# Second-pass output products of a gated MLP: from plain matmuls to Strassen's seven

## Chip, cores and metric

One NeuronCore of a Trainium2 chip runs the whole program; inputs and outputs lie in HBM. The metric is the device time of one execution in microseconds; the kernel before took 1191.15 us (median of three runs, 1191.02 to 1193.08).

## What is computed

The reference is block-causal attention (8 batches, 8 heads, 576 positions, head size 64) whose output, as 4608 tokens of 512, goes through a gated MLP with d_ff 1536:

```python
scores = (1.0 / np.sqrt(D)) * np.matmul(q, k.transpose(0, 1, 3, 2))
mask = pos[:, None] // 64 >= pos[None, :] // 64
attn = softmax(np.where(mask, scores, -1e9))        # over the last axis
x = np.matmul(attn, v).transpose(0, 2, 1, 3).reshape(B * S, H * D)
gate = 1.0 / (1.0 + np.exp(-(x @ w_gate)))
val = x @ w_val
out = (gate * val @ w_out).astype(np.float32)
```

The weights arrive as float64, which the kernel reads as pairs of 32-bit words and turns into float32 itself. For accuracy every product of two float32 matrices is made of three matmuls of a high and a low part (high·high, high·low, low·high), so each operand is split: ACT makes the high part by a cast, DVE or POOL the low part by a subtraction.

## The kernel before, in words

The d_ff axis is cut in 12 chunks of 128. The first four (F1) are computed batch by batch beside attention (`mlp1`, L577 and on; `hidden` L121, `out_mm` L129), and their contribution to the output is written to `part_d` in DRAM. The other eight are computed after attention, in two passes g = 0 and 1 of four chunks each. A pass runs over six blocks of 768 tokens (NK = 6, two halves of N2 = 384).

In a block the hidden products are made by Strassen's scheme with seven products in place of eight. A `unit` (L862) is one of four combinations of column half q and gate or value; it has seven `product`s (L844) of six matmuls 128×384 (L852), and DVE adds the PSUM banks and the copied first product p1 (L868) together at L883 to L896. The value unit multiplies by one plus the tanh of the gate's half (L875, L879), which gives a quarter of h; ACT and DVE or POOL split it (`split_h`, L857, L859 and L860) into `hH2` and `hL2`.

Then `out_block` (L917) multiplies h with w_out plainly: six tiles of 128 tokens, each 12 matmuls 128×512 (L926), 72 a block. In pass 0 ACT scales the tile by one half (L935) and it is stored to `part2_d`. In pass 1 POOL adds the tiles of `part_d` and `part2_d` (L948), DVE scales the product and adds that sum (L949), and SP stores the result (L950). The last block fetches all its part sums early (`parts_load`, L900) and writes in halves at L941.

While a block runs, the x of the next is fetched (`x_load`, L715), three combinations of it are made by POOL (`x_sums`, L728) and the seven operands are split (`x_split`, L735): ACT casts (L742) and DVE subtracts (L743) four, two and one operands at a time for each of two row halves. During pass 0, `later` holds pieces of work for pass 1: combining and splitting the gate and value weights (`combine`) and splitting w_out (`wo_piece`, L705), each written to DRAM and read back at the turn of the pass.

The order on each engine is set at build time by a scheduler that simulates the program; `behind` adds constraints of order only. Each engine works through its queue in order. PSUM has two banks in `ps_m` (tiles m) and six in `ps_b` (tiles b).

Of the kernel before, what the change touches and what calls it, by code (L numbers as in the profile page):

```python
# [9 lines left out]
F32 = mybir.dt.float32  # L10
# [30 lines left out]
def attn_glu_kernel(ctx: ExitStack, tc: tile.TileContext, q, k, v, w_gate, w_val, w_out, out):  # L41
# [117 lines left out]
    with ExitStack() as s2:  # L159
# [468 lines left out]
        wo_d = dram.tile([P, 4, 2, DM], F32, name="wo_d")  # L628
# [85 lines left out]
        def x_load(k, j):  # L714

            b, o = divmod(2 * k * N2, S)
            n0 = S - o
            XB = cv.tile([P, 6, N2], F32, name="XB", bufs=2)
# [16 lines left out]
        def x_split(XBs, other=None):  # L735

            def split(a, b, src):
                for j, XB in enumerate(XBs):
                    if src == 2:
                        nc.vector.tensor_sub(out=XB[:, 2], in0=XB[:, 2], in1=XB[:, 5])  # L740
                    x = XB[:, src:src + b - a]
                    nc.scalar.copy(out=XO[j][0][:, a:b], in_=x)  # L742
                    sub = nc.vector.tensor_sub(out=XO[j][1][:, a:b], in0=x, in1=XO[j][0][:, a:b].bitcast(F32))  # L743
                    if other:
                        behind(sub.ins, other)

            split(0, 4, 0)
            split(4, 6, 4)
            split(6, 7, 2)
# [106 lines left out]

        def split_h(q, i, hH, hL, h):  # L857
            f, n = ((q, 0), (q, N2), (q + 2, 0), (q + 2, N2))[i]
            nc.scalar.copy(out=hH[:, f, n:n + N2], in_=h)  # L859
            (nc.vector if q else nc.gpsimd).tensor_sub(out=hL[:, f, n:n + N2], in0=h, in1=hH[:, f, n:n + N2].bitcast(F32))  # L860

        def unit(q, gv, w, ts, hH, hL):  # L862
# [3 lines left out]
            p1 = m2.tile([P, N2], F32, name="p1", bufs=2)  # L866
# [5 lines left out]
            def done(i, c):  # L872
# [4 lines left out]
                else:  # L877
                    h = ts[0] if i == 0 else c
                    nc.vector.scalar_tensor_tensor(out=h, in0=ts[i], scalar=1.0, in1=c, op0=ALU.add, op1=ALU.mult)  # L879
                    split_h(q, i, hH, hL, h)  # L880
# [10 lines left out]
            done(1, c12)  # L891
            done(3, c22)
            done(0, A)
# [6 lines left out]
        def parts_load(k):  # L900

            a = [x.rearrange("p a n -> p (a n)") for x in (cv.tile([P, 6, N2], F32, name="XB", bufs=2) for _ in range(2))]
            a += [cv.tile([P, 2, S], F32, name="KQ", bufs=2).rearrange("p a n -> p (a n)") for _ in range(2)]
            slots = [x[:, j * DM:(j + 1) * DM] for x in a for j in range(x.shape[1] // DM)]
            sums = {}
            n = N2 // P
            for t in (*range(n, 2 * n), *range(n)):
                r = 2 * k * N2 + t * P
                pr = [slots.pop(0) for _ in range(2)]
                for tile_, src in zip(pr, (part_d, part2_d)):  # L910
                    nc.sync.dma_start(out=tile_, in_=src[r:r + P, :])
                nc.gpsimd.tensor_add(out=pr[0], in0=pr[0], in1=pr[1])
                sums[t] = pr[0]
            return sums

        def out_block(g, k, hH, hL, wo, sums=None):
            n = N2 // P  # L917
            last_unit = last2["PE"]
            for ts in (range(n, 2 * n), range(n)):
# [11 lines left out]
                for t in ts:  # L931
                    r = 2 * k * N2 + t * P
                    ost = io.tile([P, DM], F32, name="ost2", bufs=2)
                    if g == 0:
                        nc.scalar.mul(out=ost, in_=po[t], mul=0.5)  # L935
                        nc.sync.dma_start(out=part2_d[r:r + P, :], in_=ost)
                        continue
                    if sums:
                        for e, queue in enumerate((nc.sync, nc.scalar)):
                            c = slice(e * DM // 2, (e + 1) * DM // 2)  # L940
                            nc.vector.scalar_tensor_tensor(out=ost[:, c], in0=po[t][:, c], scalar=0.5, in1=sums[t][:, c],  # L941
                                                           op0=ALU.mult, op1=ALU.add)
                            queue.dma_start(out=out[r:r + P, c], in_=ost[:, c])
                        continue
                    pr = [io.tile([P, DM], F32, name=f"pr{i}", bufs=2) for i in range(2)]
                    for tile_, src in zip(pr, (part_d, part2_d)):
                        mark2("SP", nc.sync.dma_start(out=tile_, in_=src[r:r + P, :]))
                    nc.gpsimd.tensor_add(out=pr[0], in0=pr[0], in1=pr[1])  # L948
                    nc.vector.scalar_tensor_tensor(out=ost, in0=po[t], scalar=0.5, in1=pr[0], op0=ALU.mult, op1=ALU.add)  # L949
                    nc.sync.dma_start(out=out[r:r + P, :], in_=ost)  # L950
# [7 lines left out]
        x_split(early_x, sums)  # L958
# [9 lines left out]
        ps_b = s2.enter_context(tc.tile_pool(name="ps_b", bufs=6, space=PSUM, reuse_waits="tile"))  # L968
        W.update({u: wgv_tile(*u) for u in units[1:]})
# [17 lines left out]
        for n, (q, gv) in enumerate(units):  # L987
            for j in range(KC):
                def one(n=n, q=q, gv=gv, j=j):
                    st = io.tile([P, 2, 7, P], F32R, name="st")  # L990
# [3 lines left out]
        for f in range(4):  # L994
            def one(f=f):
                st = io.tile([P, 2, DM], F32R, name="sto", tag="st")
                wo_piece(1, f, st, True)
                nc.sync.dma_start(out=wo_d[:, f], in_=st.bitcast(F32))
# [8 lines left out]
        hL = hp2.tile([P, 4, 2 * N2], F32R, name="hL2")  # L1007
        for g in range(G):
            for k in range(NK):
                end = g == G - 1 and k == NK - 1  # L1010
                if not end and (g or k):
                    XBs = [x_load((k + 1) % NK, j) for j in range(KC)]
                    for XB in XBs:
                        x_sums(XB, nc.gpsimd)
                sums = parts_load(k) if end else None
                ts = {}
                gens = [unit(q, gv, W[q, gv], ts, hH, hL) for q, gv in units]
# [12 lines left out]
                if not end:  # L1030
                    x_split(XBs)
                out_block(g, k, hH, hL, wo, sums)
                if g + 1 < G:
                    do_later(k, 2)
                    if k == NK - 1:
                        assert not later
                        wo = wop.tile([P, 4, 2, DM], F32R, name="wo2")
                        nc.sync.dma_start(out=wo.bitcast(F32), in_=wo_d)
# [29 lines left out]
```

## Time and profile before

| what | value |
|---|---|
| median of three runs | 1191.15 us |
| profiled execution, its time | 1190.19 us |
| its span (first to last instruction) | 1188.3 us |
| mean granted TensorE clock | 0.995 |
| first multiplication by a tanh of pass 0 (L879) | 637.4 us |
| pass 1 (g = 1), six blocks | 907 to 1183.5 us |
| from the last output matmul's start to the end of the span | 1183.2 to 1188.3 us |

PE is TensorE's matmul stream, PEld its weight loads, which run beside it; DVE, ACT and POOL are the vector, scalar and GpSimd engines, SP issues most DMAs. A row of the timeline is start, duration, engine, line, operation, and "out<-in" in the program's tile names. Matmuls are pipelined, so how long one takes is read from start to start. A line of the chain names what held the end of the program at that time, with the count of instructions in it. A group of the trace gives its total and mean, then the engine's idle time ahead of it and what ended that.

### The profile page before, as it was taken

How to read it: one execution, taken by the hardware profiler on the slowest of the kernel's cores; microseconds unless marked ns; L12 is line 12 of the kernel's file. 1: busy time of each engine (PE TensorE's matmuls, PEld its weight loads, DVE VectorE, ACT ScalarE, POOL GpSimd, SP SyncE). 2: the span in 40 equal slices, each digit the busy share in tenths (PEclk: the TensorE clock that was granted, in tenths of full speed). 3: DMA queues.
4: the chain of work that ended last, by engine and by line, in shares of the span. 5: the costliest groups of instructions: out<-in, count | busy, mean ns of one | idle time of the engine just before them, and what ended most of it. 6: DMA issues, size and time to landing. Idle time of an engine off the chain costs nothing.

```text
span 1188.3 us, 19309 instructions
## 1 busy us (share of the span) xinstructions
PE 1155.9 (97%) x6749; PEld 975.7 (82%) x6749; DVE 762.1 (64%) x1397; ACT 620.8 (52%) x1372; POOL 355.6 (30%) x390
## 2 busy tenths in 40 slices
PE   6899999999999999999999999999999999999998
PEld 4556778778777877787889889899999998998997
DVE  4678855554555546457959976867876755746744
ACT  6777766766676667665335354453454322423421
POOL 2345523222331323134002223223122161451440
PEclk8999999999999999999999999999999999999999
DMA  8655434435434453534424245325288264263351
GB/s 190 183 136 117 108 89 100 114 75 126 101 91 106 100 128 76 119 109 128 132 63 124 89 138 204 111 94 204 66 299 294 81 195 139 76 205 101 120 177 54
DMA packets 253361, 153.34 MB, mean 129 GB/s; under 512 B 193232, under 2 KB 215248, under 8 KB 252624
## 3 DMA queue, kind: packets, MB, share of 16 engines
q1 hardware_dynamic: 241600, 132.15, 39.9%
q10 hardware_dynamic: 11280, 18.91, 4.3%
q8 instruction: 53, 0.87, 0.3%
q0 software_dynamic: 384, 1.05, 0.3%
q14 instruction: 44, 0.36, 0.1%
HBM read 104.73 MB, written 47.33 MB: 128 GB/s over the span
## 4 chain that ended last, share of the span: by engine, by line
PE 81%; DVE 7%; DMA 4%; ACT 3%; issue 2%; POOL 2%; SPq 2%; DVEq 0%; POOLq 0%; ACTq 0%
PE b L852 20%; PE m L126 14%; PE bank L253 14%; PE m L926 10%; PE m L133 7%; PE bank L257 6%; PE b L926 5%; PE bank L126 3%; DMA pr<-part_d 2%; DVE XL L743 1%; ACT P L381 1%; PE bank L133 1%; POOL pr L948 1%; PE m L257 1%; DMA out_dram<-ost 0%
## 5 line engine op out<-in xcount | busy, mean ns | idle before, releaser
L852 PE MATMUL b<-XH,w 128*128 128x384 f32 x1344 | 351.2, 336 | 6.1 <-DVE v L888 3.4
L852 PEld LDWEIGHTS b<-XH,w 128*128 128x128 f32 x1344 | 244.0, 188 | 13.0 <-DVE v L888 6.6
L852 PE MATMUL b<-XL,w 128*128 128x384 f32 x672 | 224.7, 335 | 0.0
L381 ACT ACTIVATE P<-bank,nm 128x512 f32<-128x512 f32 (+3 forms) x256 | 132.2, 531 | 72.7 <-DVE nm L378 72.7
L378 DVE TENSOR_REDUCE nm<-bank 128x2 f32<-128x1024 f32 (+3 forms) x128 | 105.4, 823 | 40.9 <-ACT P L381 37.8
L852 PEld LDWEIGHTS b<-XL,w 128*128 128x128 f32 x672 | 126.1, 188 | 1.3
L926 PE MATMUL m<-wo,hH 128*128 128x512 f32 x384 | 124.9, 391 | 0.0
L356 ACT COPY G<-bank 128x768 f32<-128x768 f32 (+3 forms) x140 | 93.4, 695 | 26.7 <-PE bank L257 25.8
L253 PE MATMUL bank<-G,VS 128*64 128x320 f32 (+4 forms) x896 | 94.5, 360 | 0.1
L133 PE MATMUL m<-wo,hH 128*128 128x512 f32 x256 | 85.4, 398 | 1.4 <-ACT ost L610 1.0
L253 PEld LDWEIGHTS bank<-G,VS 128*64 128x64 f32 x896 | 56.1, 137 | 36.8 <-issue 4.7
L875 ACT ACTIVATE g<-g 128x384 f32<-128x384 f32 x72 | 37.4, 524 | 89.6 <-DVE g L888 58.9
L926 PEld LDWEIGHTS m<-wo,hH 128*128 128x128 f32 x384 | 71.9, 188 | 13.6
L742 ACT CAST XH<-XB 128x1536 fp32r<-128x1536 f32 (+2 forms) x72 | 66.2, 938 | 32.2 <-DVE XB L740 25.6
L126 PE MATMUL m<-XH,wv 128*128 128x512 f32 x240 | 82.3, 400 | 0.0
L126 PE MATMUL m<-XH,wg 128*128 128x512 f32 x240 | 81.8, 398 | 0.0
L743 DVE TENSOR_TENSOR XL<-XB,XH 128x1536 fp32r<-128x1536 f32 (+2 forms) x72 | 77.6, 1083 | 1.6 <-ACT XH L742 1.2
L926 PE MATMUL m<-wo,hL 128*128 128x512 f32 x192 | 75.2, 392 | 0.0
L257 PEld LDWEIGHTS bank<-ident,P 128*128 128x128 f32 x560 | 65.7, 141 | 11.5 <-ACT P L381 0.7
L257 PE MATMUL bank<-ident,P 128*128 128x128 f32 x560 | 74.9, 273 | 0.1
L948 POOL TENSOR_TENSOR pr<-pr,pr 128x512 f32<-128x512 f32 x30 | 40.3, 1344 | 109.2 <-DMA pr<-part_d 107.6
L398 DVE MEMSET bank<- 64x128 f32 x64 | 10.6, 165 | 95.4 <-PE bank L253 94.7
(182 smaller groups left out, 2315.2 us busy)
## 6 DMA issues: line engine op xcount, KB each, us to landing
pr<-part_d SPq DMA_DIRECT2D x60, 256.0 KB
xT_d<-xT ACTq DMA_DIRECT2D x32, 288.0 KB
XB<-xT_d SPq DMA_DIRECT2D x16, 576.0 KB
part_d<-ost SPq DMA_DIRECT2D x36, 256.0 KB
VS<-in_v_dram SPq DMA_DIRECT2D x64, 128.0 KB
part_d<-ost ACTq DMA_DIRECT2D x32, 256.0 KB
rqk<-in_k_dram SPq DMA_DIRECT2D x108, 72.0 KB
rqk<-in_q_dram SPq DMA_DIRECT2D x108, 72.0 KB
```

What stands on the lines that cost most here:

```text
L126: mm = nc.tensor.matmul(ps, lhsT=lh, rhs=rh, start=(i == 0), stop=(i == n - 1))
L133: mm = nc.tensor.matmul(ps, lhsT=lh[:, f, t * P:(t + 1) * P], rhs=rh, start=(f == i == 0), stop=(f == F1 - 1 and i == 2))
L253: pe_last[:] = [nc.tensor.matmul(*args, **kw).ins]
L257: pe_last[:] = [nc.tensor.transpose(*args).ins]
L356: mark("ACT", nc.scalar.copy(out=dst, in_=src))
L378: mark("DVE", nc.vector.tensor_reduce(out=nm[:, c0:c0 + 2], in_=ps[:, :, c:c + n], axis=AX.X, op=ALU.max, negate=True))
L381: mark("ACT", nc.scalar.activation(out=Pi[:, h], in_=ps[:, h, c:c + n], func=AF.Exp, bias=nm[:, c0 + h:c0 + h + 1], accum_out=sm[:, 5 * h ...
L742: nc.scalar.copy(out=XO[j][0][:, a:b], in_=x)
L743: sub = nc.vector.tensor_sub(out=XO[j][1][:, a:b], in0=x, in1=XO[j][0][:, a:b].bitcast(F32))
L852: mm = nc.tensor.matmul(ps, lhsT=lh, rhs=rh, start=(first and k == 0), stop=(k == n - 1), skip_group_check=not first)
L926: mm = nc.tensor.matmul(po[t], lhsT=lh[:, f, t * P:(t + 1) * P], rhs=rh, start=(half == 0 and i == 0), stop=(half == 1 and i == 5))
L948: nc.gpsimd.tensor_add(out=pr[0], in0=pr[0], in1=pr[1])
```

## The change

In pass 1 the output product of a block, 768×512 tokens by 512 of d_ff, is made by Strassen's seven too. Its operands are combinations: of w_out (`combine_wo`, L714, in pass 0 in place of `wo_piece`) and of h (`h_sums`, L914, in place of `split_h`). The products (`out_strassen`, L1027) are 126 matmuls 128×256 a block (L1052) in place of 72 of 128×512. Each product goes from PSUM straight into the running sum `ACC` (L1063, DVE), but the first, which ACT copies (L1082) and POOL adds.

```diff
+        def combine_wo(g, q, sub, dst):
...
+            nc.vector.tensor_sub(out=T[:, 4], in0=T[:, 1], in1=T[:, 0])
+            nc.vector.tensor_sub(out=T[:, 1], in0=T[:, 3], in1=T[:, 1])
+            nc.vector.tensor_sub(out=T[:, 5], in0=T[:, 3], in1=T[:, 4])
+            nc.vector.tensor_sub(out=T[:, 6], in0=T[:, 2], in1=T[:, 5])
+            nc.scalar.mul(out=dst[:, 0], in_=T[:, :7], mul=0.5)
+            nc.vector.scalar_tensor_tensor(out=dst[:, 1], in0=T[:, :7], scalar=0.5, in1=dst[:, 0].bitcast(F32),
+                                           op0=ALU.mult, op1=ALU.subtract)
...
+        def h_sums(q, i, hop, h, ts):
+
+            V, G_ = nc.vector, nc.vector if q else nc.gpsimd
+
+            def put(s, x, eng=V):
+                lower(hop(s, 0, q), hop(s, 1, q), x, eng)
+
+            if i == 1:
+                s1, s2 = ts[3], ts[1]
+                V.tensor_add(out=s1, in0=h[1], in1=h[3])
+                V.tensor_sub(out=s2, in0=s1, in1=h[0])
+                put(5, s2)
+                put(1, s1)
+                G_.tensor_sub(out=h[1], in0=h[0], in1=h[1])
+                put(4, h[1], G_)
+            else:
+                s = {0: 0, 2: 2, 3: 3}[i]
+                put(s, h[i], V if i == 0 else G_)
+            if i == 2:
+                V.tensor_sub(out=ts[2], in0=h[2], in1=ts[1])
+                put(6, ts[2])
```

The half that multiplies the product is now in w_out's combinations. The partial sums are added in pass 0: each tile there takes `part_d` on top before it is stored, so pass 1 loads one tensor.

```diff
-                    if g == 0:
-                        nc.scalar.mul(out=ost, in_=po[t], mul=0.5)
-                        nc.sync.dma_start(out=part2_d[r:r + P, :], in_=ost)
-                        continue
...
-                    nc.gpsimd.tensor_add(out=pr[0], in0=pr[0], in1=pr[1])
-                    nc.vector.scalar_tensor_tensor(out=ost, in0=po[t], scalar=0.5, in1=pr[0], op0=ALU.mult, op1=ALU.add)
-                    nc.sync.dma_start(out=out[r:r + P, :], in_=ost)
+                    nc.sync.dma_start(out=pr, in_=part_d[r:r + P, :])
+                    nc.scalar.mul(out=ost, in_=po[t], mul=0.5)
+                    nc.gpsimd.tensor_add(out=ost, in0=ost, in1=pr)
+                    nc.sync.dma_start(out=part2_d[r:r + P, :], in_=ost)
...
+            for th, nh in ((0, 1), (1, 1), (1, 0)):
+                for u in range(2):
+                    add(acc[u][th][nh], p1[u], nc.gpsimd)
```

For x in pass 1 there is less room: nine slots in two tiles `xa` (five and four), and p1 in what is left of the second. Combinations are made in place, so each operand is split by itself in an order that frees slots (`x_split_late`, L772): 14 casts and 14 subtractions of 384, three of them and four of the combinations on POOL (`G_`), in pieces that `out_strassen` takes between its products.

```diff
+            put(1, 2, Y[:, 2])
+            put(1, 5, Y[:, 0])
+            V.tensor_sub(out=X[:, 2], in0=X[:, 2], in1=X[:, 4])
+            G_.tensor_sub(out=Y[:, 1], in0=Y[:, 3], in1=Y[:, 1])
+            yield
+            put(0, 1, X[:, 1])
+            G_.tensor_sub(out=Y[:, 2], in0=Y[:, 2], in1=Y[:, 0])
+            put(1, 1, Y[:, 1], G_)
+            put(0, 3, X[:, 3])
+            yield
+            put(1, 3, Y[:, 3], G_)
...
+                    if g:
+                        X = XBs[0]
+                        nc.gpsimd.tensor_sub(out=X[:, 4], in0=X[:, 1], in1=X[:, 0])
+                        nc.gpsimd.tensor_sub(out=X[:, 1], in0=X[:, 3], in1=X[:, 1])
```

How the queues change at a block boundary of pass 1, first on TensorE, where the units end (tile b) and the out product begins. Before:

```order
L852 MATMUL b_10714<-XL1_6191,w11_9176 128x384
L852 MATMUL b_10714<-XH1_6190,w11_9176 128x384
L926 MATMUL m_10802<-wo2_9302,hH2_6840 128x512
L926 MATMUL m_10802<-wo2_9302,hL2_6841 128x512
L926 MATMUL m_10802<-wo2_9302,hH2_6840 128x512 x2
L926 MATMUL m_10802<-wo2_9302,hL2_6841 128x512
```

And now, in another block (T in the prediction is the start of the product whose last two matmuls head these rows; `hs` holds the high and low parts of the combinations five to seven of h, `wo2` and `wo3` those of w_out):

```order
L909 MATMUL b_10000<-XL1_6191,w11_9188 128x384
L909 MATMUL b_10000<-XH1_6190,w11_9188 128x384
L1052 MATMUL b_10083<-wo2_9324,hH2_6842 128x256
L1052 MATMUL b_10083<-wo2_9324,hL2_6843 128x256
L1052 MATMUL b_10083<-wo2_9324,hH2_6842 128x256 x2
L1052 MATMUL b_10083<-wo2_9324,hL2_6843 128x256
```

The out product follows the units as before, in narrower matmuls, of which a row half of one product takes up to six.

On DVE at that place, from the last adds of the units on. Before:

```order
L879 SCALAR_TENSOR_TENSOR v22_9922<-g22_9862,v22_9922 128x384
L879 SCALAR_TENSOR_TENSOR v12_9920<-g12_9860,v12_9920 128x384
L743 TENSOR_TENSOR XL0_6189<-XB_9710,XH0_6188 128x1536
L896 TENSOR_TENSOR v21_9921<-b_9902,p1_9904 128x384
L743 TENSOR_TENSOR XL1_6191<-XB_9713,XH1_6190 128x1536
L860 TENSOR_TENSOR hL2_6841<-v22_9922,hH2_6840 128x384
L740 TENSOR_TENSOR XB_9710<-XB_9710 128x384
L860 TENSOR_TENSOR hL2_6841<-v12_9920,hH2_6840 128x384
```

Now:

```order
L979 TENSOR_TENSOR g21_9959<-b_9936,xa_9329 128x384
L923 TENSOR_TENSOR g22_9960<-v12_10017,v22_10019 128x384
L770 TENSOR_TENSOR XL0_6189<-xa_9328,XH0_6188 128x384
L770 TENSOR_TENSOR hL2_6843<-v22_10019,hH2_6842 128x384
L924 TENSOR_TENSOR g12_9958<-g22_9960,t11_9995 128x384
L927 TENSOR_TENSOR v12_10017<-t11_9995,v12_10017 128x384
L959 SCALAR_TENSOR_TENSOR v21_10018<-g21_9959,v21_10018 128x384
L770 TENSOR_TENSOR hL2_6843<-g22_9960,hH2_6842 128x384
L770 TENSOR_TENSOR hs_9333<-g12_9958,hs_9331 128x384
L933 TENSOR_TENSOR g21_9959<-v21_10018,g12_9958 128x384
```

Between the last products and the low halves of h stand the combinations of h (L923, L924, L927, L933) and single low halves of x in place of the large ones.

On POOL, from the last low half of h of the first column half on. Before:

```order
L860 TENSOR_TENSOR hL2_6841<-v21_10200,hH2_6840 128x384
L948 TENSOR_TENSOR pr0_10452<-pr0_10452,pr1_10453 128x512
L948 TENSOR_TENSOR pr0_10499<-pr0_10499,pr1_10500 128x512
L948 TENSOR_TENSOR pr0_10507<-pr0_10507,pr1_10508 128x512
L729 TENSOR_TENSOR XB_10522<-XB_10522 128x384
L732 TENSOR_TENSOR XB_10522<-XB_10522 128x384
```

Now:

```order
L770 TENSOR_TENSOR hL2_6843<-v21_9883,hH2_6842 128x384
L797 TENSOR_TENSOR xa_9329<-xa_9329 128x384
L792 TENSOR_TENSOR xa_9329<-xa_9329 128x384
L770 TENSOR_TENSOR XL1_6191<-xa_9329,XH1_6190 128x384 x2
L800 TENSOR_TENSOR xa_9329<-xa_9329 128x384
L770 TENSOR_TENSOR XL1_6191<-xa_9329,XH1_6190 128x384
L1063 TENSOR_TENSOR xa_9328<-xa_9329,xa_9328 128x256
L1063 TENSOR_TENSOR acc_6704<-xa_9329,acc_6704 128x2x256
L1185 TENSOR_TENSOR xa_9328<-xa_9328 128x384
L1186 TENSOR_TENSOR xa_9328<-xa_9328 128x384
```

POOL's adds of part sums are gone from this pass; in their place it makes part of x's combinations and low halves and adds p1 into the sums, and the first combinations of the x after that (L1185, L1186) stand among those adds.

More of the change, by code (lines that the diff above doesn't have):

```diff
@@ L745, in split, with lower, x_split_late, put @@
                         behind(sub.ins, other)
-            split(0, 4, 0)
-            split(4, 6, 4)
-            split(6, 7, 2)
+            for part in ((0, 4, 0), (4, 6, 4), (6, 7, 2)):
+                split(*part)
+                yield
+        def lower(hi, lo, h, eng):
+            nc.scalar.copy(out=hi, in_=h)
+            return eng.tensor_sub(out=lo, in0=h, in1=hi.bitcast(F32))
+        def x_split_late(X, Y):
+            V, G_ = nc.vector, nc.gpsimd
+            turn = last2["DVE"]
+            def put(j, op, src, eng=V):
+                hi, lo = (XO[j][e][:, op] for e in range(2))
+                sub = lower(hi, lo, src, eng)
+                if eng is V and op in (1, 2, 3, 6):
+                    behind(sub.ins, turn)
+            put(0, 0, X[:, 0])
+            put(1, 0, Y[:, 0])
+            put(0, 4, X[:, 4])
+            G_.tensor_sub(out=Y[:, 0], in0=Y[:, 1], in1=Y[:, 0])
+            V.tensor_sub(out=X[:, 4], in0=X[:, 3], in1=X[:, 4])
+            yield
+            put(0, 5, X[:, 4])
+            put(1, 4, Y[:, 0])
+            put(0, 2, X[:, 2])
+            G_.tensor_sub(out=Y[:, 0], in0=Y[:, 3], in1=Y[:, 0])
+            yield
+            put(1, 2, Y[:, 2])
+            put(1, 5, Y[:, 0])
+            V.tensor_sub(out=X[:, 2], in0=X[:, 2], in1=X[:, 4])
+            G_.tensor_sub(out=Y[:, 1], in0=Y[:, 3], in1=Y[:, 1])
+            yield
+            put(0, 1, X[:, 1])
+            G_.tensor_sub(out=Y[:, 2], in0=Y[:, 2], in1=Y[:, 0])
+            put(1, 1, Y[:, 1], G_)
+            put(0, 3, X[:, 3])
+            yield
+            put(1, 3, Y[:, 3], G_)
+            put(0, 6, X[:, 2])
+            put(1, 6, Y[:, 2], G_)
         n = len(pairs)
@@ L898, in unit, with out_block @@
             yield
[L900 to L911, printed above, removed]
-                nc.gpsimd.tensor_add(out=pr[0], in0=pr[0], in1=pr[1])
-                sums[t] = pr[0]
-            return sums
-        def out_block(g, k, hH, hL, wo, sums=None):
+        n_out = [0]
+        def out_block(k, hH, hL, wo):
             n = N2 // P
@@ L945, in out_block @@
[L945 to L949, printed above, removed]
-                    nc.sync.dma_start(out=out[r:r + P, :], in_=ost)
+                    j = 2 * (n_out[0] % 2)
@@ L957, in attn_glu_kernel @@
             sums = sums_gv(*e, alone=done)
-        x_split(early_x, sums)
+        run(x_split(early_x, sums))
         run(mlp)
@@ L993, in attn_glu_kernel, with one @@
                 later.append(one)
[L994 to L998, printed above, removed]
+        for q, sub in itertools.product(range(2), range(2)):
+            def one(q=q, sub=sub):
+                combine_wo(1, q, sub, st)
+                nc.sync.dma_start(out=wo_d.rearrange("p e s q (b n) -> q b p (e s) n", b=2)[q, sub],
+                                  in_=st.rearrange("p e s n -> p (e s) n").bitcast(F32))
             later.append(one)
@@ L1029, in attn_glu_kernel, with wop_, hop @@
                             nc.sync.dma_start(out=W[q, gv].bitcast(F32), in_=wgv_d[n])
[L1030 to L1038, printed above, removed]
+                xs = iter(()) if end else x_split_late(*XBs) if g else x_split(XBs)
+                if g:
+                    out_strassen(k, hop, wop_, xs, end)
+                    continue
+                run(xs)
+                out_block(k, hH, hL, wo)
+                do_later(k, 2)
+                if k == NK - 1:
+                    assert not later and G == 2
+                    wo = [wop.tile([P, 2, 4, 2, DM // 2], F32R, name="wo2"),
+                          io.tile([P, 2, 3, 2, DM // 2], F32R, name="wo3", tag="st")]
+                    for x, n in zip(wo, (0, 4)):
+                        nc.sync.dma_start(out=x.rearrange("p e s q n -> p e (s q n)").bitcast(F32),
+                                          in_=wo_d[:, :, n:n + x.shape[2]].rearrange("p e s q n -> p e (s q n)"))
+                    def wop_(s, e, q):
+                        return wo[s // 4][:, e, s % 4, q]
+                    XA.extend(cv.tile([P, 6 * N2], F32, name="xa", tag="XB", bufs=2) for _ in range(2))
+                    PP.append(XA[1][:, 4 * N2:])
+                    more = [[cv.tile([P, 3, N2], F32R, name="hs", tag=t, bufs=b) for t, b in x]
+                            for x in ((("KQ", 2), ("rqk0", 1)), (("KQ", 2), ("rqk1", 1)))]
+                    main = [x.rearrange("p f (a n) -> p (f a) n", n=N2) for x in (hH, hL)]
+                    def hop(s, e, q):
+                        return main[e][:, 2 * s + q] if s < 4 else more[e][q][:, s - 4]
 _INS = ["q", "k", "v", "moe_w_gate", "moe_w_val", "moe_w_out"]
```

151 lines of the change are left out of this document (128 added, 23 removed).

## The prediction

> **What bounds the kernel now.** I read the page first, then the busy time by stretches of the second pass, then the chain of waits, then the queues of DVE and POOL around one block boundary. The page's span, engine totals and chain:
>
> ```profile
> span 1188.3 us, 19309 instructions
> PE 1155.9 (97%) x6749; PEld 975.7 (82%) x6749; DVE 762.1 (64%) x1397; ACT 620.8 (52%) x1372; POOL 355.6 (30%) x390
> PE 81%; DVE 7%; DMA 4%; ACT 3%; issue 2%; POOL 2%; SPq 2%; DVEq 0%; POOLq 0%; ACTq 0%
> ```
>
> TensorE is busy for 97% of the span and holds 81% of the chain. The change works on the second pass, the last six token blocks. Busy time by stretches, one block each, cut where the chain shows the last 24 output matmuls of a block beginning (907.02, 952.04 and so on):
>
> ```profile
> core 0: us, PE busy (x) PEld busy (x) DVE busy (x) ACT busy (x) POOL busy (x), PEclk, DMA share, GB/s
> 907.00:952.50 45.50, 45.22 (x237) 41.86 (x236) 26.03 (x44) 17.05 (x30) 13.05 (x12) 1.00 0.42 148
> 998.50:1045.00 46.50, 45.59 (x241) 42.49 (x240) 27.44 (x46) 14.37 (x26) 16.85 (x15) 1.00 0.40 131
> 1137.00:1183.50 46.50, 46.50 (x239) 42.44 (x237) 21.47 (x42) 9.20 (x19) 12.02 (x10) 1.00 0.29 98
> sum 276.50, PE 275.02 PEld 254.27 DVE 158.97 ACT 85.07 POOL 100.07; mean PE 45.84 PEld 42.38 DVE 26.50 ACT 14.18 POOL 16.68
> ```
>
> Over 276.5 us TensorE idles 1.48. The granted clock is 1.00 in each stretch. DVE has 26.5 us of work in a block of 46, POOL 16.7, ACT 14.2. So time in this pass is the number of matmuls times their spacing, unless another engine becomes late.
>
> **The change part by part.**
>
> *Matmuls.* The spacing comes from runs of the chain; for a width of 256, which this pass lacks, from attention (rows of the timeline, one matmul each second start with its twin at the same line):
>
> ```profile
> 952.04 5.48 PE m L926 x24
> 957.53 19.43 PE b L852 x111
> 309.32 0.28 PE L253 MATMUL bank<-KH,QH 64*128 64x256 f32 x2
> 309.44 0.28 PE L253 MATMUL bank<-KH,QL 64*128 64x256 f32 x2
> 309.56 0.28 PE L253 MATMUL bank<-KL,QH 64*128 64x256 f32 x2
> 313.00 0.29 PE L253 MATMUL bank<-KH,QBL 128*128 128x288 f32 x1
> 313.13 0.30 PE L253 MATMUL bank<-KL,QBH 128*128 128x288 f32 x1
> ```
>
> 512 wide: 5.48/24 = 0.228. 384 wide: 19.43/111 = 0.175, of which the lowest runs give 0.1735. 288 wide on 128 rows: 0.13. 256 wide on 64 rows: 0.12. The line through 384 and 512 (0.0545 per 128 columns) gives 0.119 at 256; I take 0.1195. Before, a block is 168 × 0.1735 + 72 × 0.228 = 29.15 + 16.4 = 45.55, which meets the 45.84 of the table. After: 29.15 + 126 × 0.1195 = 44.2. Saving 1.35 a block, **−8.0 us** over six (ends −7.3 and −8.5 by a hundredth of the spacing's error in the 256-wide row). If the 0.13 of the 288-wide rows were a floor, 126 × 0.13 = 16.4 and nothing is saved (0).
>
> [...]
>
> *Old idle time.* The 1.48 us that TensorE idles is around the output adds, which wait for part sums from DRAM; the new pass adds into sums loaded a unit earlier. **−1.0** (ends 0 and −1.5).
>
> *DVE and POOL at a block boundary.* This is the term that decides. What an operation costs DVE, by start to start in a gapless stretch, and the groups of the second pass:
>
> ```profile
> 933.93 0.55 DVE L860 TENSOR_TENSOR hL<-t,hH 128x384 fp32r<-128x384 f32 x1
> 934.39 0.55 DVE L888 TENSOR_TENSOR v<-b,v 128x384 f32<-128x384 f32 x1
> 934.86 0.55 DVE L890 TENSOR_TENSOR v<-b,v 128x384 f32<-128x384 f32 x1
> L879 DVE SCALAR_TENSOR_TENSOR v<-g,v 128x384 f32<-128x384 f32 x36 | 24.3, 680 | 0.8
> L879 DVE SCALAR_TENSOR_TENSOR t<-t,b 128x384 f32<-128x384 f32 x12 | 6.6, 546 | 0.5 <-PE b L852 0.5
> L733 POOL TENSOR_TENSOR XB<-XB 128x384 f32<-128x384 f32 x10 | 10.2, 1017 | 0.0
> L948 POOL TENSOR_TENSOR pr<-pr,pr 128x512 f32<-128x512 f32 x28 | 37.7, 1348 | 107.9 <-DMA pr<-part_d 106.2 <-DVE ost L949 1.6
> ```
>
> A 128×384 operation takes DVE 0.465 start to start and POOL 1.02. DVE's count a block goes from about 46 to 71: 18 for h, 13 for x, 28 in the units, 12 adds into the sums, some 34 us of 44. On average that fits; the boundary is where it does not. Let T be the start of the last product of the fourth unit. In the order of the changed kernel, the 43 operations of DVE from the add whose product ends 74 matmuls ahead of T (12.8 us) to the low half of the first combined h of the second column half must be done when TensorE has issued 24 more unit matmuls and 46 of the output: 24 × 0.1735 + 46 × 0.1195 = T + 9.7. That is 22.5 us for 43 × 0.47 = 20.2 us of work. Before, the out product began with rows that need only plain h; the last block-sized x operations stood beside it. What the window loses at hand-overs I read from the old chain, where DVE and ACT pass one result back and forth:
>
> ```profile
> 929.38 0.57 DVE g L890
> 929.97 0.53 ACT g L875
> 930.50 0.73 ACT XH L742
> 931.25 0.77 DVE XL L743
> ```
>
> A tanh or cast between two DVE operations costs 0.5 to 0.7. Two such round trips that nothing covers (tanh of the last gate piece, the cast of the first sum) take about 1.4, so some 0.9 us of slack is left in the window, if DVE is never held up.
>
> It is held up when POOL works. In the trace, operations of DVE with both inputs in SBUF stretch beside POOL and those with one input in PSUM do not: the group "v<-g,v" above averages 680 ns, its twin "t<-t,b", which reads PSUM, 546. Single cases, of DVE and POOL:
>
> ```profile
> 859.24 0.99 DVE L689 TENSOR_TENSOR cT<-cT 128x128 f32<-128x128 f32 x1
> 860.15 0.28 DVE L690 TENSOR_TENSOR cT<-cT 128x128 f32<-128x128 f32 x1
> 860.46 0.99 DVE L691 TENSOR_TENSOR cT<-cT 128x128 f32<-128x128 f32 x1
> 860.16 1.15 POOL L732 TENSOR_TENSOR XB<-XB 128x384 f32<-128x384 f32 x1
> 812.34 2.90 POOL L729 TENSOR_TENSOR XB<-XB 128x384 f32<-128x384 f32 x1 [22.17 <-DMA XB<-xT_d]
> 813.87 0.48 DVE L691 TENSOR_TENSOR cT<-cT 128x128 f32<-128x128 f32 x2
> ```
>
> At 860.46 a 0.28 us operation of DVE takes 0.99 beside a POOL add; at 812.34 it is POOL that takes 2.90 for 1.02 of work, until DVE's run ends at 814.35. Either one waits, and DVE loses less where it runs without a gap.
>
> [...]
>
> In the old second pass POOL was busy 100.07 of 276.5 us, 36%, and there a two-input operation of DVE lost 0.68 − 0.546 = 0.13 us on average. The window has 30 of them: 30 × 0.13 = 3.9 us, less the slack of 0.9: **a stall of 3.0 us a boundary**. Two things pull at it. POOL has up to 12 operations in the window (six for x, four for h, two adds of p1), about 12 us or 54% of it; at 0.13 × 54/36 the loss would be 5.9 and the stall 5.0. And DVE's run is nearly gapless, in which POOL waits, as at 812.34. The ends come from following both queues operation by operation: if POOL always gives way, TensorE waits 0 to 0.5; if the two take strict turns, 1.8 at T, for the add that frees a PSUM bank, and 3.6 at the low half of h, 5.4 together; if POOL gets in only where DVE reads PSUM or waits, 3.6. I take 3.0, since the group of 36 stands nearest: the same engines and kinds of operations. TensorE works in order and has no other matmul to put in, so the stall is time. Five boundaries have x to split for a next block: **+15** (0 to +27, with 18 for the 3.6). The sixth has not: **+0.5** (0 to 1).
>
> *First pass.* Each output tile is now scaled by ACT, added to the first partial sum by POOL (36 × 1.3 us) and stored; the slot of the tile comes free later. ACT already waits for such slots:
>
> ```profile
> 816.92 0.60 ACT L935 ACTIVATE ost<-b 128x512 f32<-128x512 f32 x1 [2.46 <-DMA part_d<-ost]
> 821.32 0.60 ACT L935 ACTIVATE ost<-m 128x512 f32<-128x512 f32 x1 [1.64 <-DMA part_d<-ost]
> ```
>
> Another 1.3 us on a wait of 1.6 to 2.5 delays the PSUM evacuations, and the tanh and casts queued behind them on ACT, by about as much; by the order, TensorE needs those banks 2 to 3 us after. **+1.5** in all (0 to 6 × 1.5 = 9). The combining of w_out (four pieces of some 3 us on DVE and ACT) lies under a DVE that is half idle there; uncovered it would be 12 us.
>
> *Turn and tail.* At the turn of the pass w_out's seven combinations (3.5 MB) and 1.3 MB of sums are loaded under the four units (29 us); at the 299 GB/s that the page's slices reach it is 16 us: nothing. The end is one add and a store as before: nothing, ±0.5.
>
> **Sum**, against the profiled execution of 1190.19 (0.96 below the median of the runs, inside their spread): 1190.2 − 8.0 − 1.0 + 15 + 0.5 + 1.5 = **1198.2 us**. Without the stall s of a boundary it is 1183.2 + 5 s.
>
> **The rivals**, told apart by s. About 0.2%, 2.4 us, is what a measurement can tell here; so s under 0.9 is faster, over 1.9 slower.
>
> - *DVE keeps up* (the other side). POOL is the one that waits, DVE's run being gapless in the window, and the slack covers the rest: s near 0 to 0.9, **1183.2** to 1187.7. For it: the row at 812.34, and that low-half operations of DVE stood at 0.55 in most blocks before. Against it: POOL's own results (the last x combinations) are then late by what it waited, and the casts on ACT behind them too. It decides when DVE loses under 1.8 us in a window. Chance 0.33.
> - *Forecast*: s from 1.9 to 4.1, 1192.7 to 1203.7. Chance 0.37.
> - [...] Chance for s over 4.1 in sum 0.20.
> - *In between*, s from 0.9 to 1.9: no difference, 1188 to 1192.5. Chance 0.10.
> - *No gain on TensorE*: 256-wide matmuls at 0.13, for which only the 288-wide rows speak and against which the 0.12 rows do. It adds 8 us to whatever s gives; 0.05 inside the cases above, moved to the slower side.
>
> **How the numbers follow.** Faster 0.33 and the lower edge of "in between": 0.34; same 0.10; slower 0.37 + 0.20 less that edge: 0.56. The likeliest case gives 1198.2. Its own range is 1192.7 to 1203.7; for 8 in 10 it has to hold most of the first rival, from 1183.0, and half of the third, to 1211.0.
>
> **What would show it.** In the second pass of the changed kernel TensorE's busy time should fall to about 44.3 a block, with 0.12 between 256-wide matmuls. A wait of TensorE for DVE's low halves of h, some 3 us long in all, should appear once a block, five times, with DVE running without a gap ahead of it and its two-input operations of 128×384 averaging near 0.68, those with PSUM near 0.55. If those averages stay near 0.55 and the waits are under a microsecond, the first rival is right. [...] If the first pass grows by more than 3 us, the term for its slots was wrong.

## The result, and the profile after

The changed kernel takes **1225.89 us** (median of five, 1224.11 to 1227.9) against 1191.15: a ratio of 1.0288, 95% interval 1.0273 to 1.0304. It was forecast slower, 1198.2; it lost 34.7 us where 7 were forecast, and lies above the range, which ended at 1211.0. The page of the changed kernel's profiled execution, span, engines and chain:

```profile
span 1224.1 us, 20194 instructions
PE 1162.6 (95%) x7073; PEld 993.5 (81%) x7073; DVE 875.0 (71%) x1552; ACT 648.0 (53%) x1460; POOL 429.1 (35%) x441
PE 70%; DVE 19%; DMA 4%; issue 3%; ACT 2%; SPq 2%; POOL 0%; DVEq 0%; ACTq 0%; POOLq 0%
```

TensorE's share of the chain falls from 81 to 70%, DVE's rises from 7 to 19. The span can be cut at three starts of matmuls: the first of the units, the last of the plain output products of pass 0, and the last of all.

| | first unit | last plain output of pass 0 | last output | pass 0 | pass 1 |
|---|---|---|---|---|---|
| before | 625.8 | 912.1 | 1183.2 | 286.3 | 271.1 |
| changed | 626.3 | 920.7 | 1219.7 | 294.4 | 299.0 |

Pass 0 is longer by 8.1 us, pass 1 by 27.9; the rest of the 35.8 us of span is the start (+0.5) and the tail (−0.7). Busy time of the changed kernel by stretches, a block of pass 0, its last block, and blocks 1, 2 and 5 of pass 1 (counted from 0):

```profile
core 0: us, PE busy (x) PEld busy (x) DVE busy (x) ACT busy (x) POOL busy (x), PEclk, DMA share, GB/s
727.00:773.10 46.10, 46.02 (x242) 42.75 (x241) 34.09 (x55) 21.20 (x36) 23.05 (x19) 1.00 0.48 160
867.00:915.60 48.60, 45.31 (x230) 41.85 (x229) 44.56 (x79) 21.66 (x37) 19.10 (x15) 0.96 0.91 331
968.00:1020.00 52.00, 45.91 (x297) 44.52 (x297) 44.41 (x72) 19.41 (x42) 22.61 (x19) 1.00 0.27 92
1020.00:1072.00 52.00, 47.81 (x293) 46.63 (x292) 44.32 (x71) 19.40 (x42) 22.80 (x19) 0.93 0.27 91
1176.00:1219.70 43.70, 43.70 (x299) 43.70 (x297) 32.18 (x59) 13.16 (x27) 12.02 (x10) 1.00 0.23 77
```

The last block, which has no x to split, takes 43.7 us with TensorE busy throughout: the matmuls are as cheap as forecast. Each of the five before it takes 52.0, the first 52.4, with TensorE idle for up to 6.5 us and DVE busy for 42 to 44. DVE runs without a gap from the last gate piece to the low halves of h, but its operations are long. From the timeline of DVE and POOL in one such window (an "x5" row is five operations that touch, 2.4 us at 0.465 each):

```profile
984.18 1.41 DVE L923 TENSOR_TENSOR g<-v,v 128x384 f32<-128x384 f32 x1
998.64 4.06 DVE L770 TENSOR_TENSOR XL<-xa,XH 128x384 fp32r<-128x384 f32 x5
1007.74 1.62 DVE L924 TENSOR_TENSOR g<-g,t 128x384 f32<-128x384 f32 x1
984.17 1.01 POOL L770 TENSOR_TENSOR hL<-v,hH 128x384 fp32r<-128x384 f32 x1 [16.69 <-ACT hH L769]
998.68 1.38 POOL L770 TENSOR_TENSOR XL<-xa,XH 128x384 fp32r<-128x384 f32 x1 [0.85 <-ACT XH L769]
1000.62 1.20 POOL L800 TENSOR_TENSOR xa<-xa 128x384 f32<-128x384 f32 x1 [0.56 <-DVE XL L770]
1007.36 1.58 POOL L1063 TENSOR_TENSOR acc<-xa,acc 128x512 f32<-128x512 f32 x1
```

Each long operation of DVE in these rows lies beside one of POOL: the five of 998.64 lose 1.7 us to two operations of POOL. The groups of the five blocks say the same, two-input operations first, then one that reads PSUM:

```profile
L770 DVE TENSOR_TENSOR XL<-xa,XH 128x384 fp32r<-128x384 f32 x55 | 40.5, 771 | 0.0
L770 DVE TENSOR_TENSOR hs<-g,hs 128x384 fp32r<-128x384 f32 x20 | 16.8, 841 | 0.0
L924 DVE TENSOR_TENSOR g<-g,t 128x384 f32<-128x384 f32 x10 | 10.9, 1090 | 0.2
L972 DVE TENSOR_TENSOR g<-b,g 128x384 f32<-128x384 f32 x10 | 5.5, 550 | 6.4 <-PE b L909 6.4
```

Over all of DVE's 128×384 groups of these blocks, the time above 0.55 us per operation sums to 8.9 us a block (0.9 in the kernel before, its larger operations on x aside). For TensorE, the waits of one block:

```profile
PE b L909 <- DVE v L972: 1.7, 1, 1.7
PE b L1052 <- ACT hs L769: 1.7, 1, 1.7
PE b L1052 <- DVE hL L770: 1.7, 2, 1.3
PE b L909 <- ACT hH L769: 1.0, 1, 1.0
```

Together they are 6.1 us. The first is the wait at T for the add that frees a bank; the second, and 0.4 us of the third, are for the cast and the low half of a combined h. These are the places that the prediction named. The other 1.3 us of the third are for the low half of the last plain part of h, which stands behind the combinations on DVE. For ACT's copy of the next first product, which would have been the sign of late adds of p1 on POOL, TensorE does not wait in this pass.

### The profile page after: what moved, and what is told of

Read it like the earlier page. It is cut to its first block, busy times and chain, and to the rows that moved or that the text cites. A ratio compares the mean times of both kernels' runs of the same rounds, so it can differ in the third digit from the quotient of the medians.

```text
span 1224.1 us, 20194 instructions
## 1 busy us (share of the span) xinstructions
PE 1162.6 (95%) x7073; PEld 993.5 (81%) x7073; DVE 875.0 (71%) x1552; ACT 648.0 (53%) x1460; POOL 429.1 (35%) x441
## 4 chain that ended last, share of the span: by engine, by line
PE 70%; DVE 19%; DMA 4%; issue 3%; ACT 2%; SPq 2%; POOL 0%; DVEq 0%; ACTq 0%; POOLq 0%
PE b L909 15%; PE m L126 14%; PE bank L253 13%; PE m L133 7%; PE bank L257 6%; PE m L995 5%; PE b L1052 4%; DVE XL L770 3%; PE bank L126 3%; PE b L995 2%; DVE v L959 1%; DMA xa<-xT_d 1%; DVE hL L770 1%; PE m L1052 1%; DVE XL L760 1%
## 5 line engine op out<-in xcount | busy, mean ns | idle before, releaser
L909 PE MATMUL b<-XH,w 128*128 128x384 f32 x1344 | 355.0, 338 | 22.2 <-DVE v L972 14.5
L1007 POOL TENSOR_TENSOR acc<-acc 128x512 f32<-128x512 f32 x36 | 57.3, 1602 | 145.7 <-ACT acc L1006 140.2
L133 PE MATMUL m<-wo,hH 128*128 128x512 f32 x256 | 85.4, 398 | 1.4 <-ACT ost L610 1.0
L322 POOL TENSOR_SCALAR KQ<-KQ 128x128 f32<-128x128 f32 x24 | 13.3, 554 | 180.0 <-DVE KQ L285 180.0
L151 POOL TENSOR_TENSOR hL<-h,hH 128x512 fp32r<-128x512 f32 x28 | 36.1, 1291 | 100.1 <-ACT hH L150 98.7
L995 PE MATMUL m<-wo,hH 128*128 128x512 f32 x192 | 63.4, 396 | 0.0
L504 POOL TENSOR_TENSOR XL<-xT,XH 128x576 fp32r<-128x576 f32 x32 | 47.0, 1470 | 39.1 <-ACT XH L499 37.2
L133 PEld LDWEIGHTS m<-wo,hH 128*128 128x128 f32 x256 | 47.9, 188 | 11.6 <-ACT ost L610 1.2
```

What stands on the lines that cost most here:

```text
L133: mm = nc.tensor.matmul(ps, lhsT=lh[:, f, t * P:(t + 1) * P], rhs=rh, start=(f == i == 0), stop=(f == F1 - 1 and i == 2))
L909: mm = nc.tensor.matmul(ps, lhsT=lh, rhs=rh, start=(first and k == 0), stop=(k == n - 1), skip_group_check=not first)
L995: mm = nc.tensor.matmul(po[t], lhsT=lh[:, f, t * P:(t + 1) * P], rhs=rh, start=(half == 0 and i == 0), stop=(half == 1 and i == 5))
L1007: nc.gpsimd.tensor_add(out=ost, in0=ost, in1=pr)
```

## The experiments

The theories. **A**: DVE and POOL wait for each other at SBUF reads. **B**: DVE has too many operations in the window, contended or not. **C**: x's load and POOL's adds of p1, by way of ACT's copy, hold the block. **D**: the order puts x ahead of h. For pass 0, **P** (the adds of part_d) and **Q** (the order at its start, w_out's combinations at its end). Unless more is said, a time is that of one execution, and stands beside 1188 to 1192 for the kernel before on the same chip; "pass 0" and "pass 1" are cut as in the table above. The traces show how far single executions can be trusted. Up to 908 us, some 12 us before the end of pass 0, every engine has the same order in the changed kernel and in eight of the versions below (those that leave the adds and w_out's sums of pass 0 as they are), and their pass 0 takes from 294.4 to 297.5 us. A difference of less than 3 us in pass 0 is therefore not shown by one execution.

**POOL only writes.**

```diff
-            G_.tensor_sub(out=Y[:, 0], in0=Y[:, 1], in1=Y[:, 0])
+            G_.memset(Y[:, 0], 0.0)
...
-                eng.tensor_add(out=dst, in0=src, in1=dst)
+                if eng is nc.gpsimd:
+                    eng.memset(dst, 0.0)
```

> The changed kernel, but in pass 1 every operation of POOL (combinations and low halves of x and h, adds of p1, first sums of the next x) only writes its output, as a memset of the same tile; what they would compute is left out, DVE's and ACT's work is unchanged. Theory A (DVE and POOL wait for each other at the SBUF inputs, about 8.9 us of DVE time a block in the trace of the changed kernel): DVE's two-input 128x384 operations go back to 0.55 us on average, the five blocks of 52.0 us shorten by 6 to 7.7 to 44.5-46, the time is 1188-1196. Theory B (DVE simply has too many operations in the window): the averages fall a little but the blocks stay at 50 us or more, the time is 1216 or more.

1192.4 us, as A said; pass 1 262.7, from 299.0. A group of DVE and a block from its trace:

```profile
L772 DVE TENSOR_TENSOR XL<-xa,XH 128x384 fp32r<-128x384 f32 x55 | 29.0, 552 | 1.7 <-ACT XH L769 1.7
1014.00:1058.00 44.00, 43.78 (x290) 43.46 (x290) 35.20 (x71) 18.93 (x42) 7.67 (x19) 1.00 0.30 102
```

With the same 71 operations on DVE a block takes 44 us and TensorE is all but full. B falls. It is also the clean measure of the matmuls: pass 1 is 8.4 us shorter than before.

**All of it on DVE** in pass 1.

```diff
-            V, G_ = nc.vector, nc.gpsimd
+            V, G_ = nc.vector, nc.vector
...
-                    add(acc[u][th][nh], p1[u], nc.gpsimd)
+                    add(acc[u][th][nh], p1[u])
```

> The changed kernel, but in pass 1 all that POOL did for x, h, p1 and the next x's first sums is done by DVE: 19 more operations a block on DVE, POOL idle. Theory A (mutual waiting): it loses 8.9 us a block of waiting and gains about 12 operations of 0.47 in the window from the last gate piece to the last low half of h (5.6 us), so blocks of about 49-51 us and 1212-1222 in all. Theory B (too many operations on DVE): blocks of 57 us or more, 1250 or more.

1221.8 us, pass 1 292.4, as A said. The waiting is gone and the operations have come in its place. First a group of DVE, then the sums of the windows of the five blocks, here and in the changed kernel:

```profile
L770 DVE TENSOR_TENSOR XL<-xa,XH 128x384 fp32r<-128x384 f32 x70 | 37.3, 552 | 0.0
sum 253.90, PE 238.03 PEld 231.07 DVE 217.68 ACT 102.26 POOL 6.39; mean PE 47.60 PEld 46.21 DVE 43.54 ACT 20.45 POOL 1.28
sum 260.40, PE 234.13 PEld 226.60 DVE 219.47 ACT 100.50 POOL 119.21; mean PE 46.83 PEld 45.32 DVE 43.90 ACT 20.10 POOL 23.84
```

Seventy low halves cost DVE 37.3 us where 55 had cost 40.5. With nineteen more operations a block DVE is busy for 43.5 us, with POOL's help for 43.9: the stretch that POOL's work brought had cost DVE about what doing that work costs. Pass 1 is 6.6 us shorter.

**No x split in pass 1.**

```diff
-                xs = iter(()) if end else x_split_late(*XBs) if g else x_split(XBs)
+                xs = iter(()) if g else x_split(XBs)
```

> The changed kernel, but in pass 1 x is not split anew: the next block's x is loaded and its first two sums are made, the casts, combinations and low halves of x are left out and the old operands are used again. Theory A and B agree that DVE's 13 operations and POOL's seven are gone from the window: TensorE should be left as in the last block, 43.7 to 45 us a block, 1184-1192 in all. A third theory (C: the load of x and POOL's adds of p1, on which ACT's copy of the next first product waits, hold the block): blocks stay at 49 us or more.

1194.4 us, 2.4 above the stated 1184 to 1192. Pass 1 is 266.3; its blocks take 45 to 45.6, against the stated 43.7 to 45, and the rest of the miss is pass 0 (295.1), for which no theory here has a term. A block, and the waits of ACT's copy for POOL's adds of p1:

```profile
1012.50:1058.00 45.50, 45.50 (x307) 45.50 (x306) 31.35 (x59) 13.25 (x28) 10.94 (x10) 1.00 0.22 74
ACT xa L948 <- POOL acc L1063: 29.6, 4, 13.0
```

ACT waits for these adds as it did, and TensorE is full, so this part of C falls. The loads of x are not tested here: nothing reads the old x any more, and all of them are issued by 959 us. But in the run in which POOL only writes they are issued from 953 to 1090 us, block by block, POOL waits for them, and the block takes 44; so C falls for them too.

**x's low halves behind h's.**

```diff
-            turn = last2["DVE"]
+            turn = last2["H"]
...
                 put(6, ts[2])
+                mark2("H", last_low[0])
```

> The changed kernel with another order: DVE's low halves of x for the operands 1, 2, 3 and 6 stand behind the last low half of h. Theory D (the order is to blame: x stands ahead of h on DVE): TensorE's wait for h goes, blocks shorten by 3 us or more, under 1211. Theories A and B: the same work has to be done before the next block's units, so the wait moves to the next block's products; blocks of 51 to 55 us, 1219-1241.

1215.7 us, pass 1 285.9. It meets neither: D asked for under 1211, A and B for no gain. The order is worth 13.1 us by itself; DVE's stretched time is still 7.1 us a block. TensorE waits no more for h, as D said; over the five blocks it waits 9.9 us for the add at T and 6.4 for DVE's sums.

**Both** (all on DVE, x behind h).

> The changed kernel with both edits that took time off: in pass 1 everything of POOL is on DVE, and DVE's low halves of x for operands 1, 2, 3 and 6 stand behind the last low half of h. If the waiting for each other and the order are two separate costs, their gains add: 4 and 10, so 1210-1214. If the order only helped because POOL's operations then fell beside fewer of DVE's, 1215-1222, no better than either alone.

1204.4 us, better than either expectation: pass 1 273.1, where gains that add would give 299.0 − 6.6 − 13.1 = 279.3. Why the two together gain more is not shown.

**What POOL's reads do by themselves.** The first experiment had taken away POOL's reads, the length of its operations and its true inputs at once. Two more put these back singly: each operation of POOL as a subtraction of two constant pieces of a weight tile, or as three memsets.

```diff
+        def fill(dst):
...
+            return nc.gpsimd.tensor_sub(out=dst, in0=a, in1=b)
```

> As the run in which POOL only writes, but each of its operations in pass 1 is a subtraction of two constant pieces of a weight tile in SBUF: same count, outputs and lack of true inputs, about 1.0 us each again, with two reads (what they should compute is left out). Theory A (the reads hold DVE off): DVE's two-input operations average 0.7 us or more again and pass 1 goes from 262.7 back to 285-299. Theory E (what counted were ACT's and POOL's waits for true inputs and results of POOL): pass 1 stays at 262-270.

1206.5 us, pass 1 276.9. It came between the two ranges.

```diff
+            for _ in range(3):
+                ins = nc.gpsimd.memset(dst if dst.dtype == F32 else dst.bitcast(F32), 0.0)
```

> As the run in which POOL only writes, but each memset is made three times, so that POOL is busy 1.26 us per operation of 384, as long as in the changed kernel, without reading. Theory A: DVE's two-input operations stay at 0.55 us and pass 1 at 262-266. Theory F (the length of POOL's work is what counts, as what waits for its tiles comes later): pass 1 at 270 or more.

1192.6 us, pass 1 264.4, as A said. The same group of DVE, constant reads first, then three writes:

```profile
L782 DVE TENSOR_TENSOR XL<-xa,XH 128x384 fp32r<-128x384 f32 x55 | 37.9, 717 | 1.9 <-ACT XH L779 1.8
```

```profile
L777 DVE TENSOR_TENSOR XL<-xa,XH 128x384 fp32r<-128x384 f32 x55 | 28.8, 557 | 4.1 <-ACT XH L774 4.1
```

POOL busy by writing costs DVE next to nothing (0.6 us stretched a block); POOL busy by reading, at times of its own, costs it 4.8 us a block and pass 1 12.5 us against the three writes; with true inputs, as in the changed kernel, these are 8.9 and 34.6 us. So POOL's reads stretch DVE's operations; with true inputs they do so nearly twice as much. That this is because POOL is then released by the very results that DVE has just written, in the middle of DVE's run, is argued from the timeline; DVE's order differs a little between these kernels, and no run moved POOL's operations in time alone.

**Partial sums in pass 0, in the kernel before.**

```diff
                         nc.scalar.mul(out=ost, in_=po[t], mul=0.5)
+                        nc.gpsimd.tensor_add(out=ost, in0=ost, in1=pr)
...
-                    nc.gpsimd.tensor_add(out=pr[0], in0=pr[0], in1=pr[1])
```

> The kernel before with one part of the change alone: in pass 0 each output tile takes part_d on top (POOL) before it is stored, and pass 1 loads one partial sum and has no add on POOL. Theory P (the first pass's 8.6 us are the price of these adds: slots that come free later, ACT held up): pass 0 longer by 4 to 9 us, pass 1 shorter by 0 to 1.5, 1193-1200. Theory Q (they come from the new order at the start of the pass and from w_out's combinations at its end): pass 0 longer by 0 to 2, 1188-1192.

1190.9 us (median of ten), ratio 0.9996 (0.9979 to 1.0013): no difference, as Q said. This part alone is free in the old order; in the traced execution pass 0 takes 287.8 us, 1.5 more than in the kernel before, and pass 1 269.7, 1.4 less.

**Pass 0 without the adds**, and their loads of `part_d`, and **without w_out's sums**. First:

```diff
-                    nc.sync.dma_start(out=pr, in_=part_d[r:r + P, :])
...
-                    nc.gpsimd.tensor_add(out=ost, in0=ost, in1=pr)
```

> The changed kernel with part_d left out of the sums: pass 0 neither loads nor adds it. Theory P: pass 0 (its last 24 output matmuls start at 915.6) ends 6 us or more earlier, 1217-1220 in all. Theory Q: it ends within 3 us of where it did, 1222-1226.

1221.7 us, between the ranges of P and Q; pass 0 289.6 instead of 294.4. Then, with the split of four quarters in place of seven operands:

```diff
-            nc.vector.tensor_sub(out=T[:, 4], in0=T[:, 1], in1=T[:, 0])
...
-            nc.scalar.mul(out=dst[:, 0], in_=T[:, :7], mul=0.5)
+            nc.scalar.mul(out=dst[:, 0, :4], in_=T[:, :4], mul=0.5)
```

> The changed kernel with w_out's combinations left out: pass 0 still turns w_out into float32 and splits the four plain quarters of a piece, the four sums of a piece and the split of three more quarters are left out, so pass 1 multiplies by what was in the store. Theory Q: the last block of pass 0 loses its 4.3 us, the time falls by 3 to 5, 1220-1223. Theory P: within 1.5 of the changed kernel.

1220.8 us, in Q's range, but not for Q's reason alone: pass 0 is 292.9, 1.5 less, where Q has its last block lose 4.3, and pass 1 is 296.1, 2.9 less. So in the changed kernel the adds with their loads are 4.8 us of pass 0's 8.1, which is clear of the spread; P was right in kind there, and wrong for the old order. What the sums cost in pass 0 is not clear of the spread. One more difference is at the start of the pass. On ACT in the changed kernel the copy of a first product (L948) stands behind a conversion of w_out that waits for its load, and TensorE waits for the copy:

```profile
634.05 0.67 ACT L650 ACTIVATE cT<-raw 128x512 f32<-128x512 f32 x1 [1.20 <-DMA raw<-in_moe_w_out_dram]
634.62 0.84 ACT L948 COPY st<-b 128x384 f32<-128x384 f32 x2
PE b L909 <- ACT st L948: 2.4, 1, 2.4
```

In the kernel before, the same two copies started at 627.10 and 630.16, and TensorE does not wait for them. The second stands in its chain (start, us, what):

```profile
630.16 0.49 ACT p L868
```

The first unit matmul had started within 0.5 us of the same time (625.8 and 626.3). What is copied there is the same in both kernels; the build-time order had moved the copy.

**Repairs.** Adds by DVE from PSUM in pass 0 and two sums of x back on POOL:

```diff
-                    nc.scalar.mul(out=ost, in_=po[t], mul=0.5)
-                    nc.gpsimd.tensor_add(out=ost, in0=ost, in1=pr)
+                    nc.vector.scalar_tensor_tensor(out=ost, in0=po[t], scalar=0.5, in1=pr, op0=ALU.mult, op1=ALU.add)
```

> On top of the run with all on DVE and x behind h: the first two sums of the next x go back to POOL in pass 1, and in pass 0 the output tile is scaled and added to part_d by one DVE operation that reads PSUM, in place of ACT's scaling and POOL's add. Theory A: POOL's two sums fall beside the units' PSUM operations and cost nothing, DVE loses two operations and its wait for the load (6.5 us in the pass), pass 1 falls from 273.1 to 266-271; in pass 0 the part of the 7.7 us that the adds cost (4.8 where they were left out) goes, 295.1 to 289-292. Together 1194-1200. Rival: DVE is now the engine with the most work in both passes, and its 36 more operations of 0.6 us in pass 0 show: 1202 or more.

1198.6 us, inside the stated 1194 to 1200: pass 0 292.9, 2.2 less and not the 3 to 6 expected; pass 1 272.2, above the 266 to 271.

With the adds of p1 and the two sums of x on POOL, and w_out's pieces later in the source at the start of pass 0:

```diff
+                    if g == k == 0 and n < 2:
+                        for f in ((0, 2), (1, 3))[n]:
+                            wo_piece(0, f, wo[:, f])
```

> On top of the run with all on DVE and x behind h: in pass 1 the first two sums of the next x and the adds of p1 go back to POOL; in pass 0 the four pieces of w_out are turned into operands after the first and second unit are issued, not ahead of them. Theory A (each POOL operation beside two-input operations costs DVE more than doing it itself): pass 1 longer than the 266-271 expected with p1 on DVE, by 1 us or more a block, 273 or more in all. Rival: the adds fall beside DVE's own adds, which read PSUM, and pass 1 is shorter by 1 us or more a block than with p1 on DVE. Pass 0: if the order at its start costs the 2.7 us that TensorE waits for the copy of a first product, it falls by 2 to 3.

1205.8 us: pass 1 276.5, 4.2 longer than with those adds on DVE, so in A's direction, but 0.8 a block and not the 1 or more that A stated; pass 0 296.4, no shorter. Then the later pieces together with DVE's adds and p1 on DVE:

> The run with DVE's adds in pass 0 and POOL's two sums in pass 1, and also the later w_out pieces at the start of pass 0. If the three costs of pass 0 (adds 4.8, start 2-3, combinations 1.5) are separate, pass 0 is at 286-290, pass 1 as in that run, together 1190-1197. If they are one (DVE's total work in pass 0), pass 0 stays above 291.

1195.9 us: pass 0 290.6, between the two that were stated, pass 1 273.0. But the edit to the pieces did not do what it was made for. In the traces every engine works through the same instructions in the same order as in the run of 1198.6 us: the build-time order put the pieces back in their old place, so the two are executions of one order, 2.2 us apart in pass 0 and 0.8 in pass 1. In the run before this one the order of pass 0 had not moved either. TensorE's wait for ACT's copy is there in all of them (2.2 to 2.4 us), and no run tested what it costs. 1195.9 us is the shortest time of a version that computes the whole result, and still above the kernel before on the same chip (1189.9). Last, deeper slots and another place for x:

```diff
-                    j = 2 * (n_out[0] % 2)
+                    j = n_out[0] % 5
...
+                if op in (3, 6):
+                    behind(sub.ins, last2["P1"])
```

> On top of the run with DVE's adds and the later w_out pieces in pass 0 and all but two sums on DVE in pass 1: the tiles of pass 0 are added in place in five slots instead of two pairs, so that part_d is fetched further ahead (the last block of that run waits 6 us for such a load), and DVE's last four low halves of x stand behind the second pair of p1 adds, so that ACT's copy of the next first product waits less. If DVE's order and these waits are what is left of the 6 us to the kernel before: pass 0 288-290, pass 1 268-271, 1189-1194, no slower than the kernel before. If DVE's sum of work (42 of 46 us a block) is the floor: pass 1 stays at 272-274, 1194-1198.

1199.1 us, ratio 1.0059 (1.0041 to 1.0077): slower than the kernel before, and a miss for both of the stated cases. The traced execution is the slowest of the five, 1202.4, with pass 0 292.9 and pass 1 275.9. Its first block of pass 1 now waits for w_out itself, TensorE for 0.9 us, by its chain:

```profile
930.21 8.20 DMA wo_d<-st
938.50 7.99 DMA wo<-wo_d
```

The last piece is stored late and the load of all pieces stands behind it. No version beat the kernel before. In the run of 1195.9 us DVE is busy for 42.7 to 43.8 us of each 47 in blocks 1 to 4 of pass 1, so there is little room left on it.

## Why the prediction was wrong, point by point

- *Matmuls, −8.0, and old idle, −1.0.* Right to within 0.6 to 2.3 us. With POOL only writing, pass 1 is 8.4 us shorter than before, with the longer writes 6.7. The 256-wide spacing is 0.12, by the chain of the changed kernel:

```profile
1171.35 3.60 PE b L1052 x30
```
- *DVE and POOL at a boundary, +15.* The mechanism and its place were right, the size was wrong, and this is the step that failed: "30 × 0.13 = 3.9 us, less the slack of 0.9". Measured, 37 two-input operations a block lose 8.9 us, 0.24 each. Pass 1 is 36.3 us longer than with POOL only writing, 7.3 for each of five boundaries where 3.0 were forecast; by difference 1.6 of the 8.9 were covered. The 0.13 came from another kind of block, and from one group of operations. The runs show how far it carries: with POOL's operations at times of their own (constant reads) the 37 lose 4.8 us a block, again 0.13 each, and pass 1 is 14.2 us longer than with POOL only writing, 2.8 a boundary, near the 3.0. The true inputs bring the other 22.1; how they do it stays open, as said above.
- *The end of strict turns, 5.4.* Too low as a bound. Its 1.8 at T is near the 1.7 of the trace; behind T it had 3.6, and in the block shown TensorE waits 4.4. It counted POOL's operations at their undisturbed 1.02 us; in the rows above they take up to 1.38 where they lie beside DVE's. That this is the difference is not shown. At 5.4 a boundary the time is 1183.2 + 5 × 5.4 = 1210.2 us, the nearest of the prediction's cases and still low. That the two take strict turns was the author's assumption, and no run shows it; the runs show 0.24 us lost by each of DVE's 37 two-input operations of a block, and 7.3 us a boundary.
- *What of POOL's work holds DVE up.* DVE's low halves of x average 717 ns beside POOL's constant reads, 557 beside its longer writes, 552 with POOL idle.
- *Sixth block, +0.5.* It has no stall: 43.7 us.
- *First pass, +1.5 (0 to 9).* It took 8.1, and by the prediction's own sign (more than 3 us) the term was wrong. In the old order the adds make pass 0 longer by the forecast 1.5 in one trace, and the whole kernel no longer; in the new one, leaving them and their loads out takes 4.8 off. The remaining 3.3 us have no term in the prediction: it looked for moved instructions only at the block boundaries of pass 1, and the order on ACT at the start of pass 0 had changed too. That the copy behind w_out's conversion is part of this remainder is seen in the trace (a wait of TensorE of 2.4 us) but not shown by a run, since no edit moved it.
- *The rivals.* "DVE keeps up" is out: DVE loses 8.9 us. POOL's adds of p1, by way of ACT's copy, are out as the cause: without x's split, but with ACT still waiting for these adds (29.6 us), the stall is gone (blocks of 45 to 45.6), and TensorE never waits for that copy in pass 1. "No gain on TensorE" is out: 256-wide matmuls are 0.12 apart.

## What to carry to other kernels

An operation given to POOL was not off DVE's hands by that alone: in the five blocks DVE's 128×384 operations with both inputs in SBUF averaged 0.79 us, those that read PSUM 0.55. The nineteen of a block cost DVE 8.9 us of stretch, 0.47 each, as much as doing them takes, and the pass came out longer than with all of them on DVE (299.0 against 292.4 us). A rate of contention taken from one stage was no price for another (0.13 us an operation forecast, 0.24 measured): count the pairs that will meet, and do not take a walk of strict turns with undisturbed operations for the upper end (5.4 us forecast, 7.3 measured). Look in the trace whether an edit moved what it was to move, since a scheduler can put it back. The matmuls saved on a full TensorE paid only where the window in which operands are remade held the work (pass 1 took 271.1 us before, 262.7 with POOL only writing, 299.0 as changed), so add up that window's queue first, and look at every stage for moved instructions, not only where the change is.

## What the runs showed of the hardware

The granted clock of TensorE was below 1.00 in some of the blocks in which it idles and not in others: 0.93 in the block from 1020 to 1072 of the changed kernel, 1.00 in the one before it with more idle time. Both take 52.0 us, with DVE busy for 44.3 and 44.4. TensorE's busy time rose from 45.9 to 47.8 us between them with no change in time, though no more matmuls were counted (297 and 293), so a fuller TensorE is no sign of more matmuls there.
